# A two-layer decode kernel: engine order from a small planner inside the kernel, instead of the list scheduler's

## The chip, the cores and the metric

The kernel runs on one core of a Trainium2 chip. Its time is the device time in microseconds (us) of one execution; a profile of one execution gives the "span", some 2 us shorter. Executions of one kernel agree within 1%. Engines: PE (TensorE, matmul), DVE (VectorE), ACT (ScalarE), POOL (GpSimd), SP (SyncE, which issues all loads here).

## The reference

(Shortened.) Eight sequences, one new token each. An attention block and an MLP are applied twice, with the *same* weights and the *same* caches both times. Attention sees the last 1024 tokens of the cache, 32 heads of 128.

```python
x = A_x                                           # 8 x 1 x 640
x = x + attn(layernorm(x), k_cache, v_cache, wq, wo)   # window 1024
x = x + mlp(layernorm(x), w1, b1, w2, b2)              # 640 -> 1728 -> 640, its own layernorm too
x = x + attn(layernorm(x), k_cache, v_cache, wq, wo)
x = x + mlp(layernorm(x), w1, b1, w2, b2)
```

For one sequence ("batch" below) K and V of the window take 16 MiB. All are needed twice: in layer 1, and, after that batch's MLP, in layer 2.

## The kernel before

A *unit* is K or V of one pair of heads: 128 partitions x 4 KiB, 512 KiB. There are 24 unit buffers. Per batch the kernel streams the first eight pairs (16 units) and the second eight (16 units) for layer 1. It **keeps the second sixteen units** in place for layer 2, so only the first sixteen are loaded a second time. That saves a quarter of the traffic, and means that 16 of the 24 buffers are held from their landing until the MLP chain of the batch is through. Everything else streams through eight buffers.

A K unit must be turned by DVE (1.15 to 1.25 us), four turned units are scored together, and the four buffers come free when that *score group* is done. A V unit comes free after its own *V step* (16 small matmuls, 0.43 us). A V step needs the softmax of its whole job (eight K units).

```python
class Job:                       # eight pairs of heads of one batch in one layer
    def __init__(self, b, layer, p0, n, kept): ...
l0[b]  = [Job(b, 0, 0, 8, False), Job(b, 0, 8, 8, True)]   # layer 1: streamed / streamed and kept
l1s[b] = [Job(b, 1, 0, 8, False)]                          # layer 2: streamed again
l1k[b] = [Job(b, 1, 8, 8, True)]                           # layer 2: the kept ("resident") half

def chain(b):        # attention result -> layernorm, hidden, gelu, outer -> layernorm, queries -> expand
    ...              # 17 yields
def flow(jobs):      # turn K, scores every 4, softmax, V steps, finish, project; a yield per unit
    ...
for b in range(NB):
    ...
    side = flow(l1s[b - 1])
    merge(chain(b), NCHAIN, side, steps(l1s[b - 1]))       # interleave by counting yields
    drain(side)
    side = flow(l0[b + 1])
    merge(flow(l1k[b]), steps(l1k[b]), side, 16)
    drain(side)
```

The program text only interleaves generators. The order in which instructions stand on each engine is then made by the list scheduler of the language's tile framework.

The softmax here doesn't subtract the row's maximum and nothing guards it: scores larger than these inputs give would overflow.

Of the kernel before, what the change touches and what calls it, by code (L numbers as in the profile page):

```python
# [15 lines left out]
P = 128  # L16
NB = 8
# [18 lines left out]
MANUAL = False  # L36
# [8 lines left out]
class Job:  # L45

    def __init__(self, b, layer, p0, n, kept):
        self.b, self.layer, self.p0, self.n, self.kept = b, layer, p0, n, kept
        self.k, self.v = {}, {}


@with_exitstack
def _kernel(ctx: ExitStack, tc: tile.TileContext, A_x, A_k_cache, A_v_cache, A_wq, A_wo,
            B_x, B_w1, B_b1, B_w2, B_b2, out):
    nc = tc.nc
    if MANUAL:
        ctx.enter_context(tc.manual_schedule())
# [91 lines left out]
    def layernorm(x, nb, dst, twice):  # L149
        sq = small.tile([P, NKC, nb], FP32, tag=f"ln_sq{nb}", name="ln_sq", bufs=2 if nb == 1 else 1)  # L150
        nc.vector.tensor_tensor(out=sq[:], in0=x, in1=x, op=ALU.mult)
        yield
        st = psC.tile([P, 2, NKC, nb], FP32, tag="c", name="st_ps")
        nc.tensor.matmul(st[:, 0], lhsT=ones_f[:], rhs=x, start=True, stop=True)
        nc.tensor.matmul(st[:, 1], lhsT=ones_f[:], rhs=sq[:], start=True, stop=True)
        mv = small.tile([P, 2, nb], FP32, tag=f"ln_mv{nb}", name="ln_mv", bufs=2 if nb == 1 else 1)
        nc.vector.tensor_reduce(out=mv[:], in_=st[:].rearrange("p s k b -> p s b k"),
                                axis=AX.X, op=ALU.add)
        g = 1.0 + EPS if twice else 1.0
        e = EPS * EPS if twice else EPS  # L160
        wv = small.tile([P, nb], FP32, tag=f"ln_w{nb}", name="ln_w", bufs=2 if nb == 1 else 1)
        nc.vector.scalar_tensor_tensor(out=wv[:], in0=mv[:, 0, :], scalar=-g, in1=mv[:, 0, :],
                                       op0=ALU.mult, op1=ALU.mult)
        nc.vector.tensor_scalar(out=mv[:, 1, :], in0=mv[:, 1, :], scalar1=g, scalar2=e,
                                op0=ALU.mult, op1=ALU.add)
        nc.vector.tensor_tensor(out=wv[:], in0=mv[:, 1, :], in1=wv[:], op=ALU.add)  # L166
        nc.gpsimd.tensor_tensor(out=wv[:], in0=wv[:], in1=nhalf[:, 0:nb], op=ALU.pow)  # L167
        if nb == 1:
            nc.vector.tensor_scalar(out=dst, in0=x, scalar1=mv[:, 0, 0:1], scalar2=wv[:, 0:1],  # L169
                                    op0=ALU.subtract, op1=ALU.mult)  # L170
        else:
            nc.vector.tensor_tensor(out=sq[:], in0=x, in1=mv[:, 0:1, :].to_broadcast([P, NKC, nb]),
                                    op=ALU.subtract)
            nc.vector.tensor_tensor(out=dst, in0=sq[:], in1=wv[:, None, :].to_broadcast([P, NKC, nb]),
                                    op=ALU.mult)
        yield
        yield

    def wide(nb, name):
        if nb == 1:  # L180
            return small.tile([P, NFC, 1], FP32, tag=name, name=name)
        return units[take()][:, 0:2 * NFC * nb].bitcast(FP32).rearrange("p (f b) -> p f b", b=nb)

    def mlp(xv, xbv, nb, dst):
        yT = small.tile([P, NKC, nb], BF16, tag=f"yT{nb}", name="yT", bufs=2 if nb == 1 else 1)
        yield from layernorm(xv, nb, yT[:], True)
        nc.vector.tensor_tensor(out=xbv, in0=xv, in1=b2T[:, :, None].to_broadcast([P, NKC, nb]),
                                op=ALU.add)
        h_ps = psC.tile([P, NFC, nb], FP32, tag="c", name="h_ps")
        for fc in range(NFC):  # L190
            for kc in range(NKC):
                nc.tensor.matmul(h_ps[:, fc, :], lhsT=w1_sb[:, kc, fc * P:(fc + 1) * P],  # L192
                                 rhs=yT[:, kc, :], start=(kc == 0), stop=(kc == NKC - 1))
            if fc == 6:
                yield
        hx = wide(nb, "hx")
        nc.vector.tensor_tensor(out=hx[:], in0=h_ps[:],
                                in1=b1T[:, :, None].to_broadcast([P, NFC, nb]), op=ALU.add)
        u = wide(nb, "hu")
        nc.vector.tensor_tensor(out=u[:], in0=hx[:], in1=hx[:], op=ALU.mult)  # L200
        nc.vector.tensor_scalar(out=u[:], in0=u[:], scalar1=0.044715, scalar2=1.0,
                                op0=ALU.mult, op1=ALU.add)
        nc.vector.tensor_tensor(out=u[:], in0=u[:], in1=hx[:], op=ALU.mult)
        th = wide(nb, "th")
        nc.scalar.activation(th[:], u[:], ACT.Tanh, scale=0.7978845608028654)
        g2 = small.tile([P, NFC, nb], BF16, tag=f"g2{nb}", name="g2", bufs=2 if nb == 1 else 1)
        nc.vector.scalar_tensor_tensor(out=g2[:], in0=th[:], scalar=1.0, in1=hx[:],  # L207
                                       op0=ALU.add, op1=ALU.mult)
        yield
        yield  # L210
        o_ps = psC.tile([P, NKC, nb], FP32, tag="c", name="o2_ps")
        for n in range(NKC):
            for fc in range(NFC):
                nc.tensor.matmul(o_ps[:, n, :], lhsT=w2_sb[:, fc, n * P:(n + 1) * P],  # L214
                                 rhs=g2[:, fc, :], start=(fc == 0), stop=(fc == NFC - 1))
            if n == 2:
                yield
        nc.vector.scalar_tensor_tensor(out=dst, in0=o_ps[:], scalar=0.5, in1=xbv,
                                       op0=ALU.mult, op1=ALU.add)

    def expand(qT, qd):
        e_ps = psC.tile([P, 4, H], FP32, tag="c", name="e_ps")
        for j in range(2):
            for e in range(2):
                nc.tensor.matmul(e_ps[:, 2 * j + e, :], lhsT=sel[:, 2 * j + e, :], rhs=qT,  # L225
                                 start=True, stop=True)
        for x in range(4):
            nc.vector.tensor_tensor(  # L228
                out=qd[:, x, 8:].rearrange("p (n w) -> p n w", w=16)[:, :, 0:8].rearrange(
                    "p n (u i) -> p n u i", i=4),  # L230
                in0=e_ps[:, x, :].rearrange("p (n u) -> p n u", u=2)[:, :, :, None].to_broadcast([P, NPAIR, 2, 4]),
                in1=mask4[:, None, None, :].to_broadcast([P, NPAIR, 2, 4]), op=ALU.mult)

    loads = []

    def pump(need=None):
        while loads and (need in loads or free):
            item = loads.pop(0)
            if item[0] == "w":
                item[1]()  # L240
                continue
            which, job, i = item
            s = take()
            cache, h0 = A_k_cache if which == "k" else A_v_cache, 2 * (job.p0 + i)
            nc.sync.dma_start(units[s][:], cache[job.b, h0:h0 + 2, SK - W:, :].rearrange(
                "u (m c) d -> m u (c d)", c=TOK))
            (job.k if which == "k" else job.v)[i] = s
            if item == need:
                need = None

    def k_step(job, i):
        if i not in job.k:
            pump(("k", job, i))
        if job.layer == 0 or not job.kept:
            t = units[job.k[i]][:].bitcast(U32)
            nc.vector.transpose(t, t)  # L256

    def scores(job, z):
# [16 lines left out]
        if not job.kept or job.layer == 1:  # L275
            for i in range(4 * z, min(4 * z + 4, job.n)):
                free.append(job.k.pop(i))
            pump()

    def softmax(job):  # L280
        p_s = small.tile([P, 512], BF16, tag="p_s", name="p_s")
        rs = small.tile([P, 1], FP32, tag="rs", name="rs")
        nc.scalar.activation(p_s[:], job.s_ps[:], ACT.Exp, scale=QSCALE, accum_out=rs[:])  # L283
        nc.vector.transpose(p_s[:], p_s[:])  # L284
        turned = p_s[:].rearrange("p (t w i) -> p t w i", w=8, i=4)
        sh_ps = psH.tile([P, 4, 16, 4], FP32, tag="sh_ps", name="sh_ps")
        for a in range(4):
            for i in range(4):
                nc.tensor.matmul(sh_ps[32 * i:32 * i + 32, a], lhsT=ident[:, 32 * a:32 * a + 32],  # L289
                                 rhs=turned[:, :, 0:4, i], start=True, stop=True)  # L290
# [7 lines left out]
        job.rd = small.tile([P, 2, 4, 2], FP32, tag="rd", name="rd", bufs=4)  # L298
        nc.vector.reciprocal(job.rd[:], d_ps[:].rearrange("p (a z u) -> p z a u", z=2, u=2))  # L299

    def v_step(job, i):
        if i not in job.v:
            pump(("v", job, i))
        if i == 0:
# [199 lines left out]
```

## Time and profile before

| | |
|---|---|
| time | 693.79 us median of 6 runs (692.59 to 696.29) |
| span of the profile | 690.0 us |
| bytes read | 216.25 MB: 313 GB/s on average, 406 to 417 GB/s where nothing disturbs |
| one batch ("period") in the steady part | 77 to 79 us |
| transfer time of its 48 units at 1.28 us | 61.4 us (the prediction counts 61.7) |

Five lines of the page of the kernel before: the span, busy time of the engines, the mean busy share of the DMA engines in 40 equal slices (in tenths), what they moved in each slice, and the chain of work that ended last by engine.

```profile
span 690.0 us, 21561 instructions
...
PE 491.2 (71%) x10016; PEld 314.9 (46%) x10016; DVE 308.3 (45%) x587; ACT 39.0 (6%) x115; POOL 13.8 (2%) x27
...
DMA  8999987957899778997899788997799788997760
GB/s 346 392 386 408 382 292 284 344 234 265 280 338 408 295 281 275 388 400 246 281 333 408 292 312 272 392 401 258 256 350 409 296 303 275 391 398 245 276 221 2
...
PE 34%; DMA 29%; DVE 21%; issue 10%; ACT 2%; SPq 1%; POOL 1%; POOLq 0%; ACTq 0%
```

No engine is busy all the time. The DMA row shows why the span is longer than the 530 us that 216.25 MB take at 408 GB/s: full slices (9) alternate with slices of 6 to 8, in a pattern of period 77 us. The next fence takes one such period apart: windows of 4 us in the batch whose projection starts at 380.7 us; the last three columns are PE's granted clock, the DMA share and GB/s.

```profile
core 0: us, PE busy (x) PEld busy (x) DVE busy (x) ACT busy (x) POOL busy (x), PEclk, DMA share, GB/s
...
388.70:392.70 4.00, 3.98 (x76) 1.96 (x74) 3.05 (x7) 0.21 (x1) 0.00 (x0) 0.50 0.24 56
...
408.70:412.70 4.00, 2.50 (x31) 0.89 (x28) 0.88 (x4) 0.00 (x0) 0.00 (x0) 0.50 0.71 252
...
424.70:428.70 4.00, 2.54 (x17) 0.59 (x16) 4.00 (x5) 0.00 (x0) 0.00 (x0) 0.50 0.65 244
...
440.70:444.70 4.00, 2.29 (x17) 0.58 (x15) 3.41 (x4) 0.00 (x0) 0.00 (x0) 0.50 1.02 408
```

Transfers nearly stop at 388.7, run at 56 to 85% of the full rate from 408 to 432, and are at full rate from 437 on. The DMA queue's own timeline (start, duration, engine, line, load, count) says what happened in the slow stretch:

```profile
406.10 0.54 SPq L245 DMA_DIRECT2D unit_136<-in_A_k_cache_dram  x1
410.75 0.54 SPq L245 DMA_DIRECT2D unit_125<-in_A_k_cache_dram  x1
...
421.01 0.60 SPq L245 DMA_DIRECT2D unit_119<-in_A_v_cache_dram  x1
426.79 0.54 SPq L245 DMA_DIRECT2D unit_133<-in_A_v_cache_dram  x1
```

Three of the next eight keys have gone out together (401.99 to 403.27); the other five are loaded one by one (406.10 to 417.83), each when one more V step has freed a buffer. After four V loads nothing is issued for more than 5 us (421.01 to 426.79). Over the whole run the DMA queue waited this long for matmuls that free buffers (total us, times, longest):

```profile
SPq L245 <- PE s_ps L271: 151.2, 25, 9.2
SPq L245 <- PE o_ps L308: 103.1, 60, 4.6
```

### The profile page before, as it was taken

To read this page: it belongs to the slowest core of one execution; us is meant where nothing else is said; L and a number is where in the kernel's file an instruction comes from. 1 tells how busy PE (TensorE), PEld (TensorE's weight loads), DVE (VectorE), ACT (ScalarE), POOL (GpSimd) and SP (SyncE) were. 2 spreads that over 40 slices of the span, in tenths; PEclk is the share of its full clock that TensorE was granted. 3 is DMA by queue.
4 is the path that set the end of the run, shared out by engine and by line. 5 is a ranking of instruction groups with operands and counts; after the bars stand their busy time and mean duration, and the time that the engine had idled before them with its cause. 6 is when DMAs were issued, how large, how long until landed. Compare 5 with 4: busy or idle time off the path is not lost.

```text
span 690.0 us, 21561 instructions
## 1 busy us (share of the span) xinstructions
PE 491.2 (71%) x10016; PEld 314.9 (46%) x10016; DVE 308.3 (45%) x587; ACT 39.0 (6%) x115; POOL 13.8 (2%) x27
## 2 busy tenths in 40 slices
PE   2732487778876877678867787778776777678865
PEld 1330345455543453455534453455543553455534
DVE  2605161644355616644255616644255616634252
ACT  0000000000000000000000000000000000000000
POOL 2000000000000000000000000000000000000000
PEclk9999999555555555555555555555555555555555
DMA  8999987957899778997899788997799788997760
GB/s 346 392 386 408 382 292 284 344 234 265 280 338 408 295 281 275 388 400 246 281 333 408 292 312 272 392 401 258 256 350 409 296 303 275 391 398 245 276 221 2
DMA packets 62719, 217.65 MB, mean 315 GB/s; under 512 B 6358, under 2 KB 12198, under 8 KB 61990
## 3 DMA queue, kind: packets, MB, share of 16 engines
q1 hardware_dynamic: 62630, 216.29, 84.5%
q8 instruction: 78, 1.28, 0.7%
q14 instruction: 11, 0.09, 0.0%
HBM read 216.25 MB, written 0.01 MB: 313 GB/s over the span
## 4 chain that ended last, share of the span: by engine, by line
PE 34%; DMA 29%; DVE 21%; issue 10%; ACT 2%; SPq 1%; POOL 1%; POOLq 0%; ACTq 0%
PE s_ps L271 9%; PE o_ps L308 8%; PE q_ps L369 5%; DMA unit_134<-in_A_k_cache_dram 3%; PE att L333 3%; DMA w_sb<-in_B_w_dram 3%; DMA unit_123<-in_A_v_cache_dram 3%; PE h_ps L192 3%; PE o_ps L214 3%; DMA wo_sb<-in_A_wo_dram 3%; DVE p_s L284 2%; ACT p_s L283 2%; DMA unit_119<-in_A_k_cache_dram 2%; DMA unit_118<-in_A_k_cache_dram 2%; DMA unit_117<-in_A_k_cache_dram 2%
## 5 line engine op out<-in xcount | busy, mean ns | idle before, releaser
L271 PEld LDWEIGHTS <-qd_148 128*16 128x16 bf16 x512 | 20.4, 103 | 126.6 <-issue 86.3
L284 DVE STREAM_TRANSPOSE p_s<-p_s 128x512 bf16<-128x512 bf16 x32 | 22.8, 711 | 108.7 <-ACT p_s L283 108.7
L369 PE MATMUL q_ps<-xn,wq_sb 128*128 128x1 bf16 x1280 | 37.5, 165 | 13.2 <-issue 9.6
L333 PE MATMUL att<-ot,wo_sb 128*128 128x1 bf16 x1280 | 37.4, 165 | 10.6 <-issue 6.6
L333 PEld LDWEIGHTS <-wo_sb 128*128 128x128 bf16 x1280 | 37.1, 104 | 12.0 <-issue 12.0
L369 PEld LDWEIGHTS <-wq_sb 128*128 128x128 bf16 x1280 | 35.8, 104 | 14.3 <-issue 10.1
L271 PEld LDWEIGHTS <-qd_149 128*16 128x16 bf16 x512 | 17.5, 105 | 49.1 <-issue 45.6
L283 ACT ACTIVATE p_s<-s_ps 128x512 bf16<-128x512 f32 x32 | 19.1, 597 | 362.7 <-PE s_ps L271 362.7
L324 DVE TENSOR_TENSOR ot<-o_ps,rd 128x16 bf16<-128x16 f32 x16 | 2.8, 174 | 73.6 <-PE o_ps L308 73.6
L262 PE MATMUL s_ps<-ident,mask_l 2*128 2x512 bf16 x32 | 17.8, 562 | 22.1 <-ACT p_s L283 21.3
L228 DVE TENSOR_TENSOR qd_149<-e_ps,mask_94 128x128 bf16<-128x128 f32 x32 | 7.1, 282 | 54.5 <-PE e_ps L225 54.5
L289 PEld LDWEIGHTS <-ident 128*32 128x32 bf16 x512 | 10.7, 116 | 43.6 <-issue 37.3
L192 PEld LDWEIGHTS <-w_sb 128*128 128x128 bf16 x630 | 17.5, 104 | 22.3 <-DVE yT L169 19.4
L167 POOL TENSOR_TENSOR ln_w<-ln_w,nhalf 128x1 f32<-128x1 f32 (+1 forms) x18 | 12.0, 665 | 665.2 <-DVE ln_w L166 665.2
L214 PEld LDWEIGHTS <-w_sb 128*128 128x128 bf16 x630 | 17.5, 104 | 13.6 <-DVE g_11577 L207 2.0
L192 PE MATMUL h_ps<-yT,w_sb 128*128 128x1 bf16 (+1 forms) x630 | 18.2, 166 | 6.5 <-DVE yT L169 3.7
L289 PE MATMUL sh_ps<-p_s,ident 128*32 128x64 bf16 x512 | 13.0, 237 | 8.3 <-DVE p_s L284 8.3
L299 DVE RECIPROCAL rd<-d_ps 128x16 f32<-128x16 f32 x32 | 8.2, 258 | 23.3 <-PE d_ps L297 23.2
L271 PE MATMUL s_ps<-unit_130,qd_148 128*16 128x512 bf16 x28 | 14.2, 609 | 3.9 <-DVE unit_130 L256 3.9
L271 PE MATMUL s_ps<-unit_119,qd_148 128*16 128x512 bf16 x28 | 13.4, 616 | 4.9 <-DVE unit_119 L256 4.9
L271 PE MATMUL s_ps<-unit_122,qd_148 128*16 128x512 bf16 x28 | 14.2, 609 | 3.4 <-DVE unit_122 L256 3.4
L324 DVE TENSOR_TENSOR ot_147<-o_ps,rd 128x16 bf16<-128x16 f32 x16 | 3.7, 229 | 28.6 <-PE o_ps L308 28.6
(305 smaller groups left out, 1176.4 us busy)
## 6 DMA issues: line engine op xcount, KB each, us to landing
unit_124<-in_A_v_cache_dram SPq DMA_DIRECT2D x12, 512.0 KB, 6.1
unit_116<-in_A_k_cache_dram SPq DMA_DIRECT2D x11, 512.0 KB, 9.3
unit_117<-in_A_k_cache_dram SPq DMA_DIRECT2D x11, 512.0 KB, 10.6
unit_136<-in_A_k_cache_dram SPq DMA_DIRECT2D x11, 512.0 KB, 10.2
wq_sb<-in_A_wq_dram SPq DMA_DIRECT2D x5, 1024.0 KB, 8.0
unit_119<-in_A_k_cache_dram SPq DMA_DIRECT2D x10, 512.0 KB, 10.1
unit_122<-in_A_k_cache_dram SPq DMA_DIRECT2D x10, 512.0 KB, 10.2
wo_sb<-in_A_wo_dram SPq DMA_DIRECT2D x2, 2560.0 KB, 18.1
```

The lines of the kernel that those rows point to most:

```text
L167: nc.gpsimd.tensor_tensor(out=wv[:], in0=wv[:], in1=nhalf[:, 0:nb], op=ALU.pow)
L192: nc.tensor.matmul(h_ps[:, fc, :], lhsT=w1_sb[:, kc, fc * P:(fc + 1) * P], rhs=yT[:, kc, :], start=(kc == 0), stop=(kc == NKC - 1))
L214: nc.tensor.matmul(o_ps[:, n, :], lhsT=w2_sb[:, fc, n * P:(n + 1) * P], rhs=g2[:, fc, :], start=(fc == 0), stop=(fc == NFC - 1))
L262: nc.tensor.matmul(job.s_ps[:].rearrange("p (x u) -> p x u", u=2), lhsT=mask_l[:].rearrange("k x u i -> k (x u i)"), rhs=ident[0:2, None, ...
L271: nc.tensor.matmul(s_ps[32 * a:32 * a + 16, :].rearrange("p (t c) -> p t c", c=32), lhsT=qd[:, je, o:o + 16], rhs=k[:, je // 2, je % 2], s ...
L283: nc.scalar.activation(p_s[:], job.s_ps[:], ACT.Exp, scale=QSCALE, accum_out=rs[:])
L284: nc.vector.transpose(p_s[:], p_s[:])
L289: nc.tensor.matmul(sh_ps[32 * i:32 * i + 32, a], lhsT=ident[:, 32 * a:32 * a + 32], rhs=turned[:, :, 0:4, i], start=True, stop=True)
L299: nc.vector.reciprocal(job.rd[:], d_ps[:].rearrange("p (a z u) -> p z a u", z=2, u=2))
L308: nc.tensor.matmul(job.o_ps[:, 2 * i:2 * i + 2], lhsT=v[:, c * DH:(c + 1) * DH], rhs=job.p_v[:, a, c, 2 * z:2 * z + 2], start=(i == 0 and ...
L333: nc.tensor.matmul(att[job.b][:, n:n + 1], lhsT=wo_sb[:, h, n * P:(n + 1) * P], rhs=job.ot[:, hi:hi + 1], start=(h == 0 and n == 0), stop= ...
L369: nc.tensor.matmul(q_ps[:, h:h + 1], lhsT=wq_sb[:, kc, h * DH:(h + 1) * DH], rhs=xn[:, kc, :], start=(kc == 0), stop=(kc == NKC - 1))
```

## The change

The intent: stop leaving the engine order to the list scheduler. A `Plan` in the kernel is given every piece of work as a task with an engine, an estimated time, predecessors, a rank, and the buffers that it takes and gives back. It simulates the queues, picks at each moment the ready task of lowest rank, and *emits* instructions in that order, under a manual schedule. The MLP chain has the lowest rank (goes first), and one rule that the cut below leaves out helps it further: a task outside the chain is held back while a chain task for the same engine becomes ready within half of its own time. Streamed work is ranked by the position of its load, resident work by the position of the next batch's first load.

```diff
-    if MANUAL:
-        ctx.enter_context(tc.manual_schedule())
+    ctx.enter_context(tc.manual_schedule())
...
+class Plan:
+    HOP = 0.15
+    LOAD_LATENCY = 1.9
+    def emit(self):
+        ...
+            for e in coming:
+                while idle_at[e] <= now:
+                    ok = [t for t in coming[e] if t.ready <= now and (t.take is None or room[t.take] > 0)]
+                    if e == SP:
+                        ok = [t for t in ok if loads and t is loads[0]]
+                    if not ok:
+                        break
+                    t = min(ok, key=lambda t: (t.rank, t.seq))
+                    ...
+                    t.fn()
+                    ...
+                    if e == SP:
+                        landed = max(landed, now + self.LOAD_LATENCY) + t.flow
+                        seen = landed + 0.4
...
+    plan = Plan({"unit": NUNIT, "s": 2, "p_s": 2, "h": 1, "p_v": 2, "o": 2, "ot": 2, "att": 1, "c": 2})
...   # tasks, for example:
+            last = plan.add(PE, 1.95 + (0.45 if z == 0 else 0), lambda z=z: scores(job, z),
+                            after=turned + [last, qd_ready], rank=rank("k", group[-1]),
+                            take="s" if z == 0 else None, give=("unit",) * len(group) if give else ())
...   # inside the chain (rank CHAIN = -1):
+        step(PE, 2.0, lambda: hidden(0, NFC), take="c")
+        step(DVE, 0.85, inner, give=("c",))
+        step(ACTE, 0.25, tanh)
+        step(DVE, 0.2, gate)
+        step(PE, 2.0, lambda: outer(0, NKC), take="c")
...   # wo, w1, w2 now behind all 32 loads of batch 0 (before: after 10, 16, 22, 25 of them)
+    wo_ready = [add_weights(7.0, lambda: load_wo(0, 16)), add_weights(7.0, lambda: load_wo(16, 32))]
+    w_ready = [add_weights(5.6, load_w1), add_weights(5.6, load_w2)]
```

Arithmetic, bytes, buffers and the load order of K and V stay. In the two compiled programs one period of the PE queue reads as follows, shortened (numbers are matmuls; S1, S2 scores of layer 1 and 2, V a V step of 16, sh and d two small steps of the softmax, att the output projection, LN a layernorm's sums, h, o, q hidden, outer, queries):

```
before  V S2x17 V S2x15 V sh V d | V x8 S1x32 sh d V x8 att80 S1x32 sh d V x8 att80 S2x1 LN S2x2 h70 S2x14 o70 S2x15 sh d LN V x3 q83 V q77
after   V x8 S2x32 S1x16 sh d V x6 S1x16 V x2 sh d V x8 att80 S1x32 sh d V x8 att80 LN h70 S2x16 o70 S2x16 LN sh q160 d
```

## The prediction

> **What bounds it now.** The page gives a span of 690.0 us; HBM reads are 216.25 MB, 313 GB/s on average, yet slices reach 408 GB/s. At that rate (an estimate from these two) the bytes take 530 us. No engine is the limit by its work (PE 71%, DVE 45%); the DMA queue is, and it has gaps. The chain of waits shows 77.4 us per batch (attention projections at 303.0, 380.7, 458.1, 535.6, 613.3). A period loads 48 units of 512 KiB, one per 1.28 us when undisturbed: 61.7 us, so 15.7 us are missing. In 4 us windows of the batch at 380.7 they lie in two places: 56 GB/s at 388.7 (all eight free buffers hold keys not yet scored), and 231 to 347 GB/s from 408 to 432. There the queue's timeline shows key loads issued at 406.1, 410.8, 413.5, 415.8, 417.8 and none from 421.6 to 426.8: sixteen of 24 buffers are held for the second layer's resident half, whose scores wait for the MLP chain (28.8 us here), and the V steps that free the other eight are strewn among the chain's and the resident job's matmuls.
>
> **What the change does.** Arithmetic, bytes, buffers and the load order of K and V are the same (19830 PE rows in both). Only order moves. In the compiled order, the streamed V steps come as one block of eight (8 x 0.43 = 3.4 us) right after the chain, then both resident score groups (4.4 us) together, then the next batch's first scores; the chain goes first and should take about 24 us. The loads of wo, w1, w2 move behind all 32 of batch 0.
>
> **Hand walk of one period**, with durations from the trace (score group 1.9, mask 0.5, projection 2.3, hidden and outer 2.0 each, queries 4.45, key turn 1.15, unit 1.28, about 2 from issue to first data after a gap):
> - Gap after the eight streamed K loads: the first score group is behind the hidden layer; 3.6 us stays.
> - Gap before the next batch's K loads: 2 us, as V waits for the chain's end.
> - Resident scores free eight buffers 7 us before they are needed; no gap from there.
>
> Period: 61.7 + 5.6 = 67.3 us, 10 less than now, all on the critical path, for the queue is the limit. Start (390 GB/s up to 85 us) and tail (19 us after the last V) stay. Sum: 83 us to the first chain, 352 loads x 1.28 = 451, gaps 44, tail 20: span 598, timed 601. Planned order is exact only if times are, and every queue is served in order (the Trainium skill, "TensorE: Matmul & The Clock Gate", Part 2: matmuls stay in program order), so I add 1 us per batch or less: **606 us, range 592 to 632.** Faster by over 2%: 0.96; within 2%: 0.03; slower: 0.01. The rate is the trace's; the skill's "HBM Reference" (Specifications) has about 425 GB/s for a core streaming alone, near the 409 to 417 seen here.
>
> **Right if** the period is 66 to 70 us, DMA runs at 400 GB/s or more from about 27 us after each projection, the DMA queue's waits on score and V matmuls fall from 254 us to under 150, and PE's busy time stays near 490 us.
>
> **Wrong if** key turns placed before a chain step in the DVE's order wait for loads and stretch the chain beyond 30 us; if PE's 2 us issue stalls (113.2, 250.6) hit the dense stretches; or if the small hops exceed the planner's figures, so that the queue starves behind misplaced matmuls.

## The result, and the profile after

| | before | after |
|---|---|---|
| median us | 693.88 (20 runs) | 631.66 (10 runs, 628.67 to 634.24) |
| ratio | | 0.9102, 95% interval 0.9086 to 0.9117 |
| span of the profile | 690.0 | 629.0 |
| mean period, batches 1 to 7 | 77.8 | 70.3 |
| transfer time lost in one period | 15.7 (from 380.7) | 8.1 (from 356.2) |
| transfer time lost, mean of six periods | 16.0 | 8.8 |
| of it around the first gap | 5.4 | 5.3 |
| around the second gap | 4.2 | 3.3 |
| in the rest of the period | 6.4 | 0.1 |

Ratios here and below are the mean time of one kernel's fast runs over that of the other's in the same rounds, so not quite the ratio of the medians. Periods are measured from the first DVE step after the hidden layer of one batch to that of the next. Lost transfer time is the shortfall from 409 GB/s, summed over windows of 2 us. In the last rows "first gap" is the stretch from 3 us before to 9 us after that DVE step, "second gap" the next 16 us. So the change gains almost nothing at the first gap; nearly all of the gain of a period comes from behind the second gap, where the next batch's loads went out slowly before.

The same five lines of the page, after:

```profile
span 629.0 us, 21695 instructions
...
PE 441.7 (70%) x10016; PEld 308.0 (49%) x10016; DVE 308.8 (49%) x587; ACT 39.1 (6%) x115; POOL 14.0 (2%) x27
...
DMA  7999997998799799996899799997999789997960
GB/s 283 408 410 396 377 376 267 409 407 297 268 406 406 282 338 392 407 409 245 302 409 409 295 330 403 407 407 253 352 410 408 273 310 389 409 407 268 362 252 3
...
DMA 47%; PE 28%; issue 10%; DVE 9%; SPq 5%; POOL 0%; POOLq 0%; ACT 0%; DVEq 0%; ACTq 0%
```

PE and DVE have much the same shares as before. The DMA row has more nines, and the chain that ended last is now nearly half DMA (29% before). The DMA queue's waits for matmuls are down from 254 to 176 us (the third line names a layernorm's matmul that stands right behind a score group, so the wait is probably for that group's buffers):

```profile
SPq L364 <- PE o_ps L430: 80.1, 70, 8.6
SPq L364 <- PE s_ps L385: 70.4, 28, 9.0
...
SPq L364 <- PE st_ps L243: 25.7, 8, 9.5
```

The times of that DVE step in the eight batches:

```
before  94.48 155.12 232.52 311.67 389.24 466.65 544.24 622.06
after   92.19 147.93 215.57 286.12 358.34 427.88 498.36 569.44
```

The 61.0 us of span come from four places, read from these times: 2.3 us at the start, 4.9 us in the first period (60.6 to 55.7), 45.4 us in the six others, and 8.4 us from the last chain to the end.

What stays is as plain. One period in windows of 2 us (columns as before):

```profile
354.00:356.00 2.00, 0.03 (x1) 0.00 (x0) 1.93 (x7) 0.00 (x0) 0.54 (x1) 0.50 1.00 395
356.00:358.00 2.00, 1.80 (x67) 1.80 (x68) 2.00 (x3) 0.00 (x0) 0.00 (x0) 0.50 0.67 266
358.00:360.00 2.00, 2.00 (x26) 0.63 (x23) 1.90 (x7) 0.22 (x1) 0.00 (x0) 0.50 0.04 14
360.00:362.00 2.00, 2.00 (x64) 1.49 (x57) 1.54 (x3) 0.00 (x0) 0.00 (x0) 0.50 0.07 14
362.00:364.00 2.00, 2.00 (x37) 0.85 (x33) 0.34 (x2) 0.00 (x0) 0.00 (x0) 0.50 0.88 307
...
374.00:376.00 2.00, 0.56 (x21) 0.55 (x21) 0.00 (x0) 0.00 (x0) 0.00 (x0) 0.50 0.83 274
```

and its loads:

```profile
349.15 0.53 SPq L364 DMA_DIRECT2D unit_129<-in_A_k_cache_dram  x1
360.60 0.54 SPq L364 DMA_DIRECT2D unit_133<-in_A_v_cache_dram  x1
...
372.45 0.54 SPq L364 DMA_DIRECT2D unit_133<-in_A_k_cache_dram  x1
...
377.95 0.56 SPq L364 DMA_DIRECT2D unit_129<-in_A_k_cache_dram  x1
```

The last of eight streamed K loads is issued at 349.15. The next load is issued at 360.60, eleven microseconds later, and transfers all but stop from 357 to 362. After that come the eight V loads, a small second gap at 374, and then full rate to the end of the period. The next keys are issued in one burst (372.45 to 377.95), while before the last five took 12 us: the V block frees their buffers. This period is a good one: over the six, the second gap costs 1.7 to 5.4 us of transfer (3.3 on average), the first 5.7 to 6.2 in five of them.

Why 360.60? The timeline of PE and DVE at that place (start, duration, engine, line, operation, count, and idle time before it with what ended it):

```profile
356.20 2.03 PE L297 MATMUL h_ps<-yT,w_sb 128*128 128x1 bf16 x70 [2.17 <-DVE yT L265]
...
358.16 0.60 PE L376 MATMUL s_ps<-ident,mask_l 2*128 2x512 bf16 x1
...
359.95 0.63 PE L385 MATMUL s_ps<-unit_134,qd_151 128*16 128x512 bf16 x1
...
360.51 2.02 PE L326 MATMUL o_ps<-g_6368,w_sb 128*128 128x1 bf16 x70
```

The hidden layer (2.03 us) goes ahead of the score group, because the chain has rank first; the group's last matmuls start at 359.95, and the first buffer is refilled at 360.60. PE was nearly empty from 354 to 356.

One more change shows that nobody asked for. Score matmuls alone, over the whole run, before and then after (the second number is PE's busy time in them):

```profile
0.00:690.00 690.00, 191.85 (x1024) 37.95 (x1024) 0.59 0.85 315
```

```profile
0.00:690.00 690.00, 140.81 (x1024) 31.78 (x1024) 0.68 0.82 315
```

The same 1024 matmuls keep PE busy 51 us less. The four units of a group can overlap (at 340.17 to 340.18 us four matmuls start together, each 0.59 to 0.60 us long). In the timelines, 152 of the score matmuls before and 50 after start with no other within 0.08 us; a lone one takes about as long as four together, so the 102 fewer account for about 50 us. Two things leave them alone. The list scheduler had torn groups ("S2x1", "S2x2" above). And PE reaches a group before its four keys are turned: before, at 656.47 and 657.60 us, a lone matmul has waited 0.90 and 0.54 us for a turn. The planner emits a group only when, by its own clock, all four are turned. The run e1 below, which keeps groups whole but has no planner, has 165.64 us here, so each of the two is probably worth about half. The granted clock is not the reason: one matmul takes 0.58 to 0.63 us in both.

### The profile page after: what moved, and what is told of

Same layout as the page of the kernel before. It is cut to its first block, busy times and chain, and to the rows that moved or that the text cites. A ratio compares the mean times of both kernels' runs of the same rounds, so it can differ in the third digit from the quotient of the medians.

```text
span 629.0 us, 21695 instructions
## 1 busy us (share of the span) xinstructions
PE 441.7 (70%) x10016; PEld 308.0 (49%) x10016; DVE 308.8 (49%) x587; ACT 39.1 (6%) x115; POOL 14.0 (2%) x27
## 3 DMA queue, kind: packets, MB, share of 16 engines
q8 instruction: 78, 1.28, 0.8%
## 4 chain that ended last, share of the span: by engine, by line
DMA 47%; PE 28%; issue 10%; DVE 9%; SPq 5%; POOL 0%; POOLq 0%; ACT 0%; DVEq 0%; ACTq 0%
PE s_ps L385 7%; DMA unit_118<-in_A_k_cache_dram 7%; DMA unit_133<-in_A_k_cache_dram 7%; DMA unit_119<-in_A_k_cache_dram 6%; PE o_ps L430 5%; PE q_ps L542 5%; DMA unit_135<-in_A_k_cache_dram 4%; DMA unit_127<-in_A_v_cache_dram 3%; DMA unit_127<-in_A_k_cache_dram 3%; PE o_ps L326 3%; DMA unit_126<-in_A_k_cache_dram 3%; PE h_ps L297 3%; DMA unit_119<-in_A_v_cache_dram 2%; DMA unit_130<-in_A_v_cache_dram 2%; DMA unit_141<-in_A_v_cache_dram 2%
## 5 line engine op out<-in xcount | busy, mean ns | idle before, releaser
L385 PEld LDWEIGHTS <-qd_150 128*16 128x16 bf16 x512 | 17.8, 103 | 81.5 <-issue 57.8
L454 PE MATMUL att<-ot,wo_sb 128*128 128x1 bf16 x1280 | 37.0, 165 | 26.4 <-DVE ot L445 14.2
L542 PE MATMUL q_ps<-xn,wq_sb 128*128 128x1 bf16 x1280 | 35.8, 165 | 7.0 <-issue 7.0
L297 PE MATMUL h_ps<-yT,w_sb 128*128 128x1 bf16 (+1 forms) x630 | 18.2, 166 | 29.2 <-DVE yT L265 26.4
L297 PEld LDWEIGHTS <-w_sb 128*128 128x128 bf16 x630 | 17.5, 104 | 30.0 <-DVE yT L265 15.7
L385 PEld LDWEIGHTS <-qd_151 128*16 128x16 bf16 x512 | 14.0, 114 | 32.0 <-issue 27.0
L370 DVE STREAM_TRANSPOSE unit_118<-unit_118 128x1024 uint32<-128x1024 uint32 x12 | 14.9, 1243 | 27.4 <-DMA unit_118<-in_A_k_cache_dram 27.4
L370 DVE STREAM_TRANSPOSE unit_133<-unit_133 128x1024 uint32<-128x1024 uint32 x10 | 12.4, 1239 | 18.1 <-DMA unit_133<-in_A_k_cache_dram 18.1
L385 PE MATMUL s_ps<-unit_135,qd_150 128*16 128x512 bf16 x32 | 15.1, 616 | 5.4 <-DVE unit_135 L370 5.4
## 6 DMA issues: line engine op xcount, KB each, us to landing
unit_119<-in_A_k_cache_dram SPq DMA_DIRECT2D x12, 512.0 KB, 10.2
```

Source lines behind the costliest of these rows:

```text
L297: nc.tensor.matmul(t["h"][:, fc, :], lhsT=w1_sb[:, kc, fc * P:(fc + 1) * P], rhs=t["y"][:, kc, :], start=(kc == 0), stop=(kc == NKC - 1))
L370: nc.vector.transpose(t, t)
L385: nc.tensor.matmul(s_ps[32 * a:32 * a + 16, :].rearrange("p (t c) -> p t c", c=32), lhsT=qd[:, je, o:o + 16], rhs=k[:, je // 2, je % 2], s ...
L454: nc.tensor.matmul(att[job.b][:, n:n + 1], lhsT=wo_sb[:, h, n * P:(n + 1) * P], rhs=job.ot[:, hi:hi + 1], start=(h == 0 and n == 0), stop= ...
L542: nc.tensor.matmul(t["q"][:, h:h + 1], lhsT=wq_sb[:, kc, h * DH:(h + 1) * DH], rhs=t["x"][:, kc, :], start=(kc == 0), stop=(kc == NKC - 1))
```

## The experiments

Theory A: the gain comes from *where* the buffer-freeing matmuls stand in PE's order, because the DMA queue waits for buffers. What is left is lost the same way, at places where the plan puts the chain first. Rivals: B, the list scheduler does the harm and any other order would do; C, the gain comes from the planner's bookkeeping or the place of the weights; E, the chain's length sets the period. Eleven kernels ran; all gave correct results. Medians are compared through the ratio to the kernel before where runs are of different rounds.

| run | median us | ratio to before | mean period us |
|---|---|---|---|
| the change | 631.66 | 0.9102 | 70.3 |
| e1_program_order | 707.24 | 1.0180 | 79.7 |
| e6_list_on_plan | 668.27 | 0.9638 | 76.7 |
| e2_weights_early | 634.98 | 0.9150 | 70.4 |
| e3_chain_late_pe | 617.35 | 0.8894 | 68.6 |
| e5_units22 | 682.66 | 0.9869 | 77.2 |
| e9_hidden_yields | 617.70 | 0.8922 | 68.6 |
| e10_first_chain | 630.85 | 0.9109 | 70.5 |
| e12_both | 618.26 | 0.8920 | 68.6 |
| e17_v_last | 643.69 | 0.9282 | 72.1 |
| e13_b0 | 613.80 | 0.8842 | 68.5 |
| e14_q4 | 608.61 | 0.8776 | 67.7 |

### Is it the planner's order, or only the absence of the list scheduler?

e1_program_order: the kernel before, emitted as its text stands.

```diff
-MANUAL = False
+MANUAL = True
```

> The kernel before with the list scheduler switched off and no planner: its instructions go out in the order in which its source text emits them. Theory A (the gain comes from the order that the planner chooses, because that order frees buffers before the DMA queue needs them): source order was never meant to be a schedule, so at most half of the 62 us gain appears, 660 us or more. Rival B (the list scheduler itself does the harm, by strewing V steps among the chain; any order that keeps them together will do, and the planner adds little): 645 us or less.

Measured: 707.24 us, 1.8% slower than the kernel before (95% interval of the ratio 1.0133 to 1.0227; whether that is over 2% is unclear, but B's 645 us is far off). Rival B falls: without the list scheduler and without a planner the kernel loses. This order keeps score groups whole (PE 463.9 us busy instead of 491.2), so less PE work by itself bought nothing either.

e6_list_on_plan: the changed kernel, with the list scheduler left on.

```diff
-    ctx.enter_context(tc.manual_schedule())
```

> The changed kernel with its one line that takes the list scheduler away removed: the planner still emits, but the list scheduler then reorders. In the compiled order the eight streamed V steps no longer stand as a block right after the chain, and come after the resident scores as in the kernel before. Theory A (the place of these V steps decides when the DMA queue goes on): most of the gain is lost, 665 to 695 us, and the second gap of each period (20 to 50 us after the projection) is back at 8 us or more. Rival C (the gain comes from the planner's task cuts, unit bookkeeping and place of the weights, not from the order on the engines): near 632 us.

Measured: 668.27 us, inside theory A's range. Same tasks, same cuts, same weights, only reordered: 60% of the change's gain is gone (1 - (1 - 0.9638) / (1 - 0.9102)). From 20 to 50 us after each projection 6.3 to 10.7 us of transfer are lost, 7.9 on average over the six periods, just short of the 8 that the expectation named (8.8 before, 3.4 in the changed kernel). Rival C falls for the most part. That the planner's kernel as program text still leaves the list scheduler 3.6% faster than before is also seen; which part of it does that was not separated. And e6 brings back the whole order of the list scheduler, not only the place of the V steps; the next run moves these.

e17_v_last: one dependency added, so that the V block comes after the resident scores.

```diff
         add_job(l1k[b], q2, base=base)
+        for v in l1s[b - 1].vs if b else ():
+            l1k[b].scores[-1].users.append(v)
+            v.waits += 1
```

> The changed kernel with one added dependency in the plan: the eight streamed V steps of the batch before may start only after the second layer's resident scores. In the compiled order only this changes: after the chain come both resident score groups, then the V block, instead of the V block first. Theory A (the V block's place is one of the causes of the gain): the next keys are loaded about 3 us later in each period, period 73 to 74 us, total 646 to 656 us. Rival: the resident scores free eight buffers just as well, and the V block's place is worth nothing: 629 to 634 us.

Measured: 643.69 us, period 72.1. Direction and sign are theory A's, but the size is less than expected (12.5 us by the ratios, not 14 to 24; 1.8 us a period, not 3). The loss is where it should be: the second gap grows from 3.3 to 5.3 us on average, the rest of the period is as it was (0.2 against 0.1). In the order of the trace one more thing moves than the expectation says: the next batch's first score group now stands behind six resident V steps; no loss shows there. That the resident scores free eight buffers too is a likely reason for the smaller size. The V block's place is one cause of the gain, about a fifth of it.

### Are buffers really what is short?

e5_units22:

```diff
-NUNIT = 24
+NUNIT = 22
```

> The changed kernel with 22 unit buffers instead of 24 (the planner told so), so that six instead of eight are free while sixteen are held for the second layer. Theory F (these few free buffers, not the DMA rate and not the engines, set the gaps of each period): the planner can hold only six of the eight streamed keys, the second score group falls behind the queries, each period grows by 7 to 11 us, total 680 to 710 us; nearly the whole gain of the change is gone with two buffers. Rival: buffers are not short, the gaps come from PE and the chain: under 650 us.

Measured: 682.66 us, period 77.2. Two of eight free buffers less cost 7.0 us in each period, the lower end of the expected 7 to 11, and 51 us in all: five sixths of the whole gain. DMA rate, engines and weights were untouched, though a planner with fewer buffers also chooses another order.

### What is left in each period

e3_chain_late_pe: the chain's PE tasks ranked behind the streamed job.

```diff
-            t = plan.add(eng, us, fn, after=last[0] + list(more), rank=rank, **kw)
+            t = plan.add(eng, us, fn, after=last[0] + list(more), rank=late if eng in (PE,) else rank, **kw)
...
-        step = serial([l0[b][-1].done] + list(ready_1))
+        step = serial([l0[b][-1].done] + list(ready_1),
+                      late=l1s[b - 1].loads["v", JOB - 1].pos + 0.5 if b else CHAIN)
```

> The changed kernel with the MLP chain's PE tasks ranked behind the score and V tasks of the job that streams at the time (other engines as before): the first score group goes ahead of the hidden layer and seven V steps ahead of the queries. Theory D (each period of 70.5 us still loses about 6 us because the first score group stands behind the hidden layer, and 1.6 us because V waits for the chain's end): gaps fall to about 3.5 and 0.5 us, period 66 to 67 us, total 603 to 612 us, though the chain gets 3 to 5 us longer. Rival E (the chain's length sets the period, so the chain must go first): slower than 632 us, up to 655.

Measured: 617.35 us, period 68.6. Rival E falls: the chain goes later and the kernel is 2.3% faster. The size is short of the 603 to 612 expected. The trace says why: V steps now stand ahead of the queries, PE waits there for V loads (three waits of 0.69 to 1.16 us in the batch at 480), the chain ends later, and a gap opens behind the resident scores (outside the first two gaps 1.8 us of transfer are lost in a period, 0.1 in the changed kernel).

e9_hidden_yields: only the hidden layer yields (`yields=True` gives this task the late rank of e3).

```diff
-        step(PE, 2.0, lambda: hidden(0, NFC), take="c")
+        step(PE, 2.0, lambda: hidden(0, NFC), take="c", yields=True)
```

> The changed kernel with one PE task of each chain, the hidden layer, ranked behind the streamed job; everything else of the chain first as before. In the compiled order the first score group now stands ahead of the hidden layer, four V steps stand ahead of the queries and the rest after them. Theory D (the first score group behind the hidden layer is the mis-sized gap): first gap about 3.5 instead of 6 us, period 66 to 67 us, 603 to 613 us, and a little better than the variant that let the whole chain yield (617), whose queries stood behind V steps that waited for loads. Rival: that variant's 14 us came from the V steps ahead of the queries, not from the score group; then this one, with fewer of them, is slower than 617 us.

Measured: 617.70 us, period 68.6; the same gain from one task moved. So the score group in front of the hidden layer is worth it, and the V steps ahead of the queries were not what made e3 faster. But 603 to 613 was missed again. Three windows of one period of this run, the first gap and then the second (columns as before):

```profile
350.00:352.00 2.00, 2.00 (x39) 0.94 (x32) 2.00 (x3) 0.00 (x0) 0.00 (x0) 0.50 0.31 125
...
368.00:370.00 2.00, 0.15 (x5) 0.15 (x6) 1.52 (x2) 0.00 (x0) 0.00 (x0) 0.50 0.54 211
370.00:372.00 2.00, 2.00 (x60) 1.60 (x58) 1.64 (x5) 0.00 (x0) 0.00 (x0) 0.50 0.06 16
```

The first gap has shrunk from 6.0 to 2.7 us of lost transfer (summed over 350 to 358), while the second, 1.6 in the period of the changed kernel shown above, is 4.2 us here (368 to 378). The V loads come earlier, but half of the V steps that free their buffers still stand behind the queries. This pair of periods misleads, however. In this one PE also stalls, for a reason that the profile does not show, in the middle of these V steps:

```profile
369.85 0.34 PE L430 MATMUL o_ps<-p_v,unit 128*128 128x2 bf16 x7 [2.62 <-issue]
```

Over six periods the first gap falls from 5.3 to 2.4 us, the second goes from 3.3 to 3.7, and the rest of the period from 0.1 to 0.9; the period falls by 1.6. So over half of the first gap's gain was kept. The first gap came out better than expected (3.5); the total missed mainly because the expectation took the second gap from one good period, as 1.6 us.

### The start

The first chain after the change: key turn, yT and hidden layer on DVE and PE, with the load they wait for.

```profile
79.49 0.55 POOL L260 TENSOR_TENSOR ln_w<-ln_w,nhalf 128x1 f32<-128x1 f32 x1 [71.00 <-DVE ln_w L257]
...
88.46 1.25 DVE L370 STREAM_TRANSPOSE unit_126<-unit_126 128x1024 uint32<-128x1024 uint32 x1 [9.04 <-DMA unit_126<-in_A_k_cache_dram]
89.63 0.25 DVE L265 TENSOR_SCALAR yT<-xT,ln_mv,ln_w 128x5 bf16<-128x5 f32 x1
...
90.02 2.00 PE L297 MATMUL h_ps<-yT,w_sb 128*128 128x1 bf16 x70 [11.27 <-DVE yT L265]
```

The inputs of yT were ready at 80.04 (79.49 + 0.55). It stands in the DVE queue behind a key turn which waits 9.04 us for its load, and the hidden layer waits 11.27 us. The Trainium skill, "TensorE: Matmul & The Clock Gate" (the note on engine queue depths under "Architectural detail"), says that ACT and DVE are strict FIFO; these lines agree.

e2_weights_early: the weights back at their old places.

```diff
+    early = {9: (7.0, lambda: load_wo(0, 16)), 15: (7.0, lambda: load_wo(16, 32)),
+             21: (5.6, load_w1), 24: (5.6, load_w2)}
```

> The changed kernel with wo, w1 and w2 loaded at the places of the kernel before (after 10, 16, 22 and 25 units). The start of the changed kernel shows DMA at only 301 GB/s from 80 to 100 us and its first MLP chain held behind a key turn that waits for a load (h waits 11.3 us). Theory: the late weights cause this and cost about 5 to 7 us once: 624 to 628 us, periods unchanged at 70 to 71 us. Rival: the start is bound by bytes and this moves nothing: 631 to 633 us.

Measured: 634.98 us. Both statements miss; it is 0.5% slower, though the two 95% intervals still touch (0.9112 to 0.9188 against 0.9086 to 0.9117). With the weights in between, the last V units of batch 0 land later (their V steps end at 87.6 us), and the chain starts later still. So the late weights cost nothing here; the projection and first layernorm run while they load.

e10_first_chain: hidden waits for w1, outer for w2.

```diff
-        step(PE, 2.0, lambda: hidden(0, NFC), take="c")
+        step(PE, 2.0, lambda: hidden(0, NFC), more=w1, take="c")
-        step(PE, 2.0, lambda: outer(0, NKC), take="c")
+        step(PE, 2.0, lambda: outer(0, NKC), more=w2, take="c")
```

> The changed kernel with the first chain's hidden layer waiting for w1 and its outer layer for w2, instead of the whole first chain waiting for both in the plan. In the compiled DVE order the first key turn of the second batch then stands behind the first chain's hidden layer and gate, not ahead of its normalisation. Theory G (the start lost 7 to 10 us because yT stood in the DVE queue behind a turn that waited for a load that came late): hidden layer starts at 80 to 84 us instead of 90.0, 621 to 627 us, periods unchanged. Rival (the start is bound by the bytes before the first chain, and what is won there is lost in the next wait): 630 to 633 us.

Measured: 630.85 us: no gain, theory G falls, its rival was right. The hidden layer did start at 80.54 instead of 90.02. Lines of its timeline:

```profile
80.54 2.00 PE L297 MATMUL h_ps<-yT,w_sb 128*128 128x1 bf16 x70 [1.76 <-DMA w_sb<-in_B_w_dram]
...
94.11 4.42 PE L542 MATMUL q_ps<-xn,wq_sb 128*128 128x1 bf16 x160 [2.18 <-DVE xn L265]
...
98.47 0.60 PE L376 MATMUL s_ps<-ident,mask_l 2*128 2x512 bf16 x1
...
100.91 5.70 SPq L364 DMA_DIRECT2D unit<-in_A_v_cache_dram  x8
```

The chain, early now, put its outer layer and queries ahead of the first score group, which starts at 98.47; the V loads went out at 100.91 (98.75 after the change). Ten microseconds of chain were won, and the buffers came free two microseconds later.

e12_both: e9 and e10 together.

> The edits of the two kernels before it together. If the first gap of each period and the late first chain are separate losses, their gains add: the time of the variant with the yielding hidden layer less 5 to 9 us, 596 to 607 us. If they are one loss, no better than the better of the two.

Measured: 618.26 us, ratio 0.8920 against e9's 0.8922: the two do not add; e10's edit is worth nothing here either. By the expectation's words that is one loss, but e13 shows two places with a loss of the same kind, the chain ahead of the buffer-freeing group: e9's edit leaves the first chain as it was.

e13_b0: as e12, and the first chain's queries yield to the second batch's first keys.

```diff
+                      behind=l1s[b - 1].loads["v", JOB - 1].pos + 0.5 if b
+                      else l0[1][0].loads["k", JOB - 1].pos + 0.5)
...
+            step(PE, 4.4 / 2, lambda n=n: queries(...), take=None if n else "c", yields=b == 0)
```

> The version with the yielding hidden layer (617.7 us), the first chain waiting for w1 and w2 where it uses them, and the first chain's queries ranked behind the second batch's first keys. Theory H (earlier starts of the first chain gained nothing because its queries then went ahead of the first score group, which frees the buffers; only when the score group goes first does an early start pay): first score group at about 94 us instead of 98.5, V loads issued at about 97 instead of 100.9 us, 611 to 616 us. Rival: no gain, 616 to 620 us.

Measured: 613.80 us, ratio 0.8842 against 0.8920. Theory H holds. The lines that answer to those of e10:

```profile
93.95 1.86 PE L385 MATMUL s_ps<-unit,qd 128*16 128x512 bf16 x13 [0.93 <-DVE unit L370]
...
95.43 8.60 SPq L364 DMA_DIRECT2D unit<-in_A_v_cache_dram  x7
...
95.75 4.42 PE L544 MATMUL q_ps<-xn,wq_sb 128*128 128x1 bf16 x160
```

The queries stand behind the score group, and V loads go out at 95.43 instead of 100.91.

e14_q4: in addition the queries of all chains in four tasks that yield, and a planner that expects loads later.

```diff
-    LOAD_LATENCY = 1.9
+    LOAD_LATENCY = 2.8
...
+            step(PE, 4.4 / 4, lambda n=n: queries(n * H // 4, (n + 1) * H // 4), take=None if n else "c", yields=True)
```

> The same, with the queries of every chain cut into four tasks that yield to V steps, and the planner's latency of a load raised by 0.9 us, so that it expects 4.5 us from issue to use after a gap, as the traces show. In the compiled order six V steps stand ahead of the queries and two between their quarters. If the second gap (3 to 4 us in the version with the yielding hidden layer) is due to V steps behind the queries: second gap under 2 us, 605 to 614 us. If the late chain then delays the resident scores and opens a third gap, as in the version where the whole chain yields: 614 to 620 us.

Measured: 608.61 us (607.58 to 609.93), 12.2% less time than the kernel before, and 0.8% less than e13 in the same rounds (608.61 over 613.80). It beats both kernels. The second gap is 1.9 us in the period from 344 and 3.5 us in the one from 276, so "under 2 us" was met only in part, though the total was. Over six periods it is 2.2 us on average (3.7 in e9). Its two changes were not run apart. Its page:

```profile
span 606.1 us, 21691 instructions
...
DMA  6999999999999898998899999998899999999950
```

The DMA row is now at 8 or 9 from the first slices almost to the end; about 56 us of transfer time are lost up to 585 us (77 in the changed kernel up to 600 us).

## Why the prediction was right or wrong, point by point

- **The limit** (DMA queue short of buffers, not engines): right. e5 shows it with two buffers, e1 and e3 exclude PE's work and the chain's length.
- **Where the gain comes from** (V block right after the chain, resident scores together): right in mechanism. Of the 7.2 us less transfer time lost in a period, 6.3 lie behind the second gap, where the next batch's loads went out slowly before. e6 gives most of the gain back, e17 prices the V block's place at about 12 us; how the rest divides was not tested.
- **The chain at about 24 us**: right; the projection starts at 349.98 and the expanded queries are done at 372.9, 23 us.
- **The period of 67.3 us**: the mis-sized term. Measured 70.3 on average, just above the 66 to 70 named. Two terms of the walk's sum failed. "3.6 us stays": the first gap measured 5.3 us on average, about 6 in five of six periods. By the author's account the hand walk took the landing of the last streamed key for the end of its transfer; the trace fits that. A key is seen about 10.2 us after issue, so the one issued at 349.15 landed at about 359.3, while transfers had dried up at 357.3; so the two latencies, at the end of the old stream and the start of the new one, both count. "2 us, as V waits for the chain's end": the second gap measured 1.6 in the period shown, but 3.3 on average. In three of the six periods PE stalls for 2.0 to 2.7 us among the queries (160.06, 301.60 and 513.27 are where it goes on), and there the gap is 3.7 to 5.4; in the three others it is 1.7 to 2.5. The prediction had named such stalls under "Wrong if". That they are the cause was not tested. Six periods at 3 us more are 18 of the 26 us between 606 and 631.7. The allowance of "1 us per batch or less" was meant for such errors and was too small.
- **The start at 83 us without a gap**: wrong. About 6 us of transfer are lost between 80 and 102 us. The prediction named the very hazard ("key turns placed before a chain step in the DVE's order wait for loads"); it struck the first chain (11.27 us of waiting for yT) and cost little elsewhere (PE waited 26.4 us for yT over eight chains, 11.3 of them in the first). But e10 and e13 show that its cure alone is worth nothing: the score group's place decides there too.
- **The tail of 19 us** after the last V step: right, 610.0 to 629.0 us.
- **Waits of the DMA queue under 150 us**: missed. 150.5 by the two lines named, 176 with the layernorm line.
- **PE busy near 490 us**: wrong, 441.7. More of the score matmuls overlap. The clock is not behind the speed either: two runs of the changed kernel at a granted clock of 0.60 took 633.0 and 631.1 us, the nine others, at 0.65, 628.7 to 634.2.
- **Rate**: right. From 378 us, 28 us after the projection, windows of 2 us show 387 to 422 GB/s, 408 on average, as "400 GB/s or more from about 27 us" asked. The figure of about 425 that the skill's "HBM Reference" (Specifications) gives for a core streaming alone is a little above that. The statement taken from "TensorE: Matmul & The Clock Gate", Part 2, on matmuls in program order agrees with the timeline: the score group never passed the hidden layer, though its last turn was done 2 us before it (355.97 against 358.16).
- **The total**: 631.66 lies at the upper end of 592 to 632, 606 was 4% low. That the median fell inside by 0.3 us is luck: five of the ten runs lie above 632.

What stays open: PE shows stalls of about 2 us that nothing in the profile explains (they are called "issue", for example 2.66 us at 298.94 in the changed kernel). They hit single places in each run; those over 1 us add up to 25 us of PE time in the changed kernel and 42 in e9, not all of it on the path. The two parts of e14 were not separated.

## What to carry to other kernels

Where the load queue is short of buffers, order tasks by what they free and when, not by the critical path of the arithmetic: a score group of 2 us in front of a "critical" hidden layer made this kernel 2% faster, although it made the chain later. When one gap closes, look at the next one in the same period before counting the gain; an earlier start that only let another task go first was worth nothing here (e10). And in a static order every task placed early on an in-order engine is a wait for its slowest input, so the latency that a planner assumes should be read from the trace (e14 assumes a later one and is the fastest run, but does not show that by itself). And read a gap from all periods: the one period looked at here was among the best.

## What the Trainium skill lacked or had wrong

- "DMA: Bandwidth & Descriptors", section "Issuing engines are not separate DMA queues", says that the sequencer's time to initiate a DMA is usually small relative to the DMA. That section does not say that it can last about as long as the transfers queued ahead. Issues of weights in the changed kernel, with the issue of a unit (512 KiB) at 0.54 us for comparison:

```profile
51.84 8.75 SPq L204 DMA_DIRECT2D wo_sb<-in_A_wo_dram  x2
...
70.54 8.70 SPq L212 DMA_DIRECT2D w_sb<-in_B_w_dram  x1
```

  The second line is the last 80 KB of w2, issued behind wo, w1 and the rest of w2. So the length of an issue does not follow its own size; whether the short rows (1,280 or 3,456 bytes, a unit's have 4,096) have a share was not tested. The SP queue was held for 27 us by the five issues of weights, which by estimate from their 9,440 KB and 409 GB/s take 24 us to transfer, and no load behind them could be issued.
- The same page, section "Bandwidth", has the rule to batch DMAs to 1 MiB or more for 75% of peak, from transfers that GpSimd issued (341 GB/s at 1 MB). Here loads of 512 KiB that SyncE issued, about eight in flight on one queue (10.2 us from issue to landing, one per 1.28 us), kept 409 GB/s. The rule has no word on depth.
- "DMA: Bandwidth & Descriptors" has the latency of one transfer, but no page has a figure for planning the restart of a load stream: from the free buffer's issue at 360.60 to a rate over 300 GB/s some 2 us passed, and as much again was lost at the end of the stream before, so that by estimate from these times a wait for buffers costs about 4 us more than the engines' part of it suggests.
